# Three buffers instead of two for the attention inputs, with crossbar transfers issued one quad earlier

## The chip, the cores and the metric

The kernel runs on one core of a Trainium2 chip. The metric is the device time of one execution in microseconds (us); the time given for a kernel is the median of its runs.

## What is computed

The reference is a softcapped attention followed by a two-way maxout layer and an output projection. Cut to what matters:

```python
# q, k, v: (8 images, 12 heads, 448 rows, 64 columns), float32; cap = 30
scores = (q @ k^T) / sqrt(64)
scores = cap * tanh(scores / cap)
attn   = softmax(scores)
x      = attn @ v                      # as (3584, 768): images and rows by heads and columns
g      = maximum(x @ w1, x @ w2)       # w1, w2: (768, 1024)
out    = g @ w_out                     # (3584, 768), float32
```

## The kernel before

The 96 heads are taken as 48 pairs (index i), and two pairs make a quad (index t, 24 quads of four heads; pairs 2t and 2t+1). For each quad:

- **Loads.** The loads of k and q (steps `lk`, `lq`) go through GpSimd's queue (POOL in the profile), which turns float32 into bf16 on the way, into a constant tile `kqs[t % KB]`. v is loaded by `lv` into `vp[t % VB]` and, for the last 64 rows of a head, into `vl[t % VB]`.
- **Turning.** q and k have to stand with their 64 columns on the partitions. Pairs 0 to 9 (quads 0 to 4) are turned by TensorE (step `X`). From quad 5 on, the step `cr t` issues one transposing DMA through the crossbar from the queue of SyncE (SP), from `kqs[t % KB]` into the tile `qkT` of the quad, which comes from a pool of `QB` buffers.
- **Attention.** The scores are computed by `S i j` (three blocks of rows per pair) and `L t` (the rows that are left over); ScalarE (ACT) does tanh (`T`, `TL`) and exp (`E`, `EL`); VectorE (DVE) adds up the exponentials (`A`, `B`), and `Y` to `Y3` give the inverse sums. `VL t` and `V t` multiply by v, and `N t` normalizes into `xT`.
- **The layer.** maximum(h1, h2) is written as max(h1 - h2, 0) + h2, with w1 - w2 (`wd_sb`) and with w2 @ w_out (`wm_sb`) made once at the start. A group (`O` opens it, `M` steps it, `ev` evicts it) is one PSUM bank of output. `M x y n` steps two groups at a time: group x with the upper 64 rows of the contraction and group y with the lower 64, so that two matmuls of 64 rows each run side by side in the array. Between the two halves of a group stands a hand-over: a no-operation that waits for the last matmul of the first half and on which the first matmul of the second half waits. `Hs g` puts it on SP's queue, `H g` on DVE's. `st b t` issues the output stores, also on SP's queue.

The schedule is written out by hand: the string `ORDER` lists some 2,300 steps, and each engine takes its own instructions in just this order. Waits between engines come from the data: a load into a buffer waits for the last reader of what stood there, and a queue whose first instruction waits holds up all behind it. So a load for quad t waits, with two buffers, for the crossbar transfer of quad t-2 (`kqs`) or for the values of quad t-2 (`vp`, `vl`), and a transfer `cr t` waits for the loads of quad t and for the scores of quad t-2 (`qkT`).

In `ORDER`, `cr t` stands (from quad 6 on) beside the scores of pair 2t-2, one quad ahead of the quad that reads it. The loads of a quad stand ahead of its `cr`. The place that the change touches first, in the order before:

```python
M 19 17 1; M 19 18 1; T 15 0; N 6 0; M 19 18 2; lv 8 3; O 20 1; M 20 18 2; EL 7; Hs 19; ev 17; M 20 18 1; lk 20 0;
S 15 1; M 20 19 1; N 6 1; M 20 19 1; T 15 1; M 20 19 1; lk 20 1; O 21 2; M 21 19 3; Hs 20; M 21 20 1; lq 20 0;
```

Of the kernel before, what the change touches and what calls it, by code (L numbers as in the profile page):

```python
# [14 lines left out]
P 1 0 4; P 3 0 2; OP 2 0 3; P 2 0 7; P 1 0 1; P 2 0 1; P 1 0 1; P 3 0 2; P 1 0 2; PC 2 0; PC 1 0; E 1 2 3;
E 1 0 2; TL 1; T 2 0; EL 0; S 3 0; S 2 2; P 3 0 1; W 0 2; P 3 0 1; X 4 3; T 2 2; T 3 0; VL 0; Y 0 1; V 0 0 0 3;
V 0 1 0 3; S 3 1; lwo 1 0; lwo 1 1; lq 5 0; lk 5 0; lv 1 0; lv 1 1; lk 8 0; lq 8 0; lq 7 0; lw2 4; lv 6 2; lq 6 0;
lk 7 0; lk 6 0; lw2 5; lw1 2; lw1 4; lw1 0; lv 2 0; lv 2 1; WC 0; PC 3 0; XC 4; Y1 0; Y2 0; Y3 0; N 0 0; N 0 1;
E 2 0 3; T 3 1; EL 1; E 3 0 2; OP 0 0 1; P 0 0 2; OP 2 1 2; P 2 1 2; P 0 0 1; OP 1 1 3; P 1 1 2; P 0 0 1; P 1 1 2;
# [28 lines left out]
M 15 13 2; ev 12; M 15 13 1; lk 19 1; M 15 14 2; ev 13; M 15 14 1; T 14 0; O 16 1; M 16 14 1; lq 19 0; A 6 1 1;
M 16 14 1; st 0 1; M 16 14 1; Hs 15; T 14 1; cr 8; B 6 0; M 16 15 1; S 14 2; M 16 15 1; ev 14; M 16 15 1; T 14 2;
O 17 2; M 17 15 2; H 16; M 17 15 1; B 6 1; M 17 16 2; E 13 2 3; M 17 16 1; ev 15; O 18 3; M 18 16 1; L 7; VL 6;  # L50
A 6 1 2; st 0 2; TL 7; V 6 0 0 2; V 6 1 0 2; Y 6 0; E 14 0 3; V 6 0 2 3; V 6 1 2 3; Y1 6; S 15 0; M 18 16 1;
lv 8 0; M 18 16 1; Y2 6; M 18 17 1; Y3 6; M 18 17 1; lv 8 1; M 18 17 1; O 19 0; M 19 17 2; ev 16; Hs 18; lv 8 2;
M 19 17 1; M 19 18 1; T 15 0; N 6 0; M 19 18 2; lv 8 3; O 20 1; M 20 18 2; EL 7; Hs 19; ev 17; M 20 18 1; lk 20 0;
S 15 1; M 20 19 1; N 6 1; M 20 19 1; T 15 1; M 20 19 1; lk 20 1; O 21 2; M 21 19 3; Hs 20; M 21 20 1; lq 20 0;
ev 18; M 21 20 1; S 15 2; S 16 0; ev 19; M 21 20 1; T 15 2; O 22 3; M 22 20 1; lk 21 0; M 22 20 1; A 7 0 1; Hs 21;
# [723 lines left out]
```

## Time and profile before

| what | value |
|---|---|
| device time, median of 3 runs | 328.46 us (328.15 to 328.82) |
| span of the profiled execution, first to last instruction | 326.9 us |
| median less the span | 1.56 us |
| mean granted TensorE clock | 0.998 |
| busy: PE, ACT, DVE, POOL | 320.2, 281.1, 240.1, 162.2 us |
| crossbar transfers, time from issue to landing | 19, from 4.2 to 10.0 us, median 6.7 |

The profile comes from one execution, and its own device time is not among the three runs; its span is what stands for it, and the difference of 1.56 us to the median holds what lies around the span and whatever that execution did otherwise. PE is TensorE's matmuls and PEld its weight loads, which run beside matmuls. SPq and POOLq are the DMA queues of SP and POOL. In rows of the timeline and of the chain, the first number is the start in us from the span's start and the second is the length in us. The label `qkT<-kqs` marks a crossbar transfer, `kqs<-in_k_dram` and `kqs<-in_q_dram` the loads of k and q, `vp<-in_v_dram` and `vl<-in_v_dram` those of v. The row "DMA to landing" gives the time from the start of the issuing instruction to the last completion.

### The profile page before, as it was taken

To read this page: it belongs to the slowest core of one execution; us is meant where nothing else is said; L and a number is where in the kernel's file an instruction comes from. 1 tells how busy PE (TensorE), PEld (TensorE's weight loads), DVE (VectorE), ACT (ScalarE), POOL (GpSimd) and SP (SyncE) were. 2 spreads that over 40 slices of the span, in tenths; PEclk is the share of its full clock that TensorE was granted. 3 is DMA by queue.
4 is the path that set the end of the run, shared out by engine and by line. 5 is a ranking of instruction groups with operands and counts; after the bars stand their busy time and mean duration, and the time that the engine had idled before them with its cause. 6 is when DMAs were issued, how large, how long until landed. Compare 5 with 4: busy or idle time off the path is not lost.

```text
span 326.9 us, 9772 instructions
## 1 busy us (share of the span) xinstructions
PE 320.2 (98%) x4138; PEld 184.5 (56%) x4138; DVE 240.1 (73%) x422; ACT 281.1 (86%) x278; POOL 162.2 (50%) x237
## 2 busy tenths in 40 slices
PE   7999999999999999999999999999999999999994
PEld 3454545545656664565565565556466556557662
DVE  3346899987997778987897788968878779773201
ACT  5999999999999999999999999999999999921120
POOL 7357584568772772764774474478448311000000
PEclk9999999999999999999999999999999999999999
DMA  8999999899999999999999999999999963013033
GB/s 179 174 202 185 269 256 112 92 140 116 221 188 98 134 182 191 102 99 175 163 176 108 208 114 181 128 140 182 183 116 101 201 156 45 2 50 98 0 98 96
DMA packets 134508, 46.28 MB, mean 142 GB/s; under 512 B 112321, under 2 KB 129473, under 8 KB 134465
## 3 DMA queue, kind: packets, MB, share of 16 engines
q0 software_dynamic: 94592, 25.02, 78.3%
q1 hardware_dynamic: 39424, 19.99, 31.1%
q8 instruction: 32, 0.52, 0.6%
q10 hardware_dynamic: 448, 0.66, 0.5%
q14 instruction: 12, 0.09, 0.1%
HBM read 47.78 MB, written 11.01 MB: 180 GB/s over the span
## 4 chain that ended last, share of the span: by engine, by line
PE 93%; DMA 3%; POOL 1%; DVE 1%; issue 0%
PE mm L645 61%; PE s L514 9%; PE s L606 9%; PE mm L431 5%; DMA w2b<-in_moe_w_dram 3%; PE s L528 2%; PE s L600 2%; PE mm L573 2%; PE mm L640 1%; POOL kqs L321 1%; PE mm L458 1%; PE mm L566 1%; PE mm L416 0%; DVE xT L621 0%; POOL w2b L366 0%; DVE xT L618 0%
## 5 line engine op out<-in xcount | busy, mean ns | idle before, releaser
L519 ACT ACTIVATE e<-s 128x896 bf16<-128x896 f32 x144 | 125.5, 927 | 5.7 <-PE s L514 5.2
L536 ACT ACTIVATE e<-e 128x1792 bf16<-128x1792 bf16 (+2 forms) x72 | 122.7, 1709 | 0.0
L645 PE MATMUL mm<-wo_sb,gT 64*128 64x384 bf16 x864 | 115.2, 323 | 0.0
L645 PE MATMUL mm<-wm_sb,xT 64*128 64x384 bf16 x648 | 102.2, 323 | 0.0
L645 PE MATMUL mm<-xT,wd_sb 64*128 64x448 bf16 x768 | 97.5, 349 | 0.0
L328 POOL DMA_DIRECT2D kqs<-in_k_dram x76 | 54.7, 722 | 56.1 <-DMA qkT<-kqs 50.9
L645 PEld LDWEIGHTS <-gT 64*128 64x128 bf16 x864 | 58.6, 94 | 25.5 <-issue 1.1
L645 PEld LDWEIGHTS <-wd_sb 64*128 64x128 bf16 x768 | 48.8, 94 | 26.7 <-issue 2.1
L645 PEld LDWEIGHTS <-xT 64*128 64x128 bf16 x648 | 50.3, 94 | 18.5 <-issue 0.2
L514 PE MATMUL s<-qkT 64*128 64x448 bf16 x288 | 52.7, 352 | 0.2 <-DVE xT L618 0.2
L352 POOL DMA_DIRECT2D vp<-in_v_dram x48 | 30.5, 639 | 32.6 <-PE s L514 23.5
L666 DVE TENSOR_SCALAR gT<-mm 128x448 bf16<-128x448 f32 x64 | 38.9, 617 | 8.7 <-PE mm L645 7.6
L328 POOL DMA_DIRECT2D kqs<-in_q_dram x38 | 35.1, 924 | 5.7 <-issue 2.5
L606 PE MATMUL s<-e,vp 128*32 128x448 bf16 x576 | 36.1, 354 | 0.0
L548 DVE TENSOR_TENSOR esum<-e 128x896 bf16<-128x896 bf16 x42 | 25.9, 617 | 9.1 <-ACT e L536 9.1
L621 DVE TENSOR_TENSOR xT<-s,inv 64x448 bf16<-64x448 f32 x48 | 29.9, 622 | 1.7 <-PE s L606 0.8
L548 DVE TENSOR_TENSOR esum<-esum,e 128x896 bf16<-128x896 bf16 x42 | 26.2, 623 | 5.9 <-ACT e L536 4.8
L514 PEld LDWEIGHTS <-qkT 64*128 64x128 bf16 x288 | 18.5, 94 | 20.1 <-issue 12.0
L700 ACT COPY osb<-mm 128x384 f32<-128x384 f32 x10 | 4.8, 479 | 26.9 <-PE mm L645 26.7
L702 DVE COPY osb<-mm 128x384 f32<-128x384 f32 x44 | 23.3, 554 | 6.2 <-PE mm L645 5.7
L553 DVE TENSOR_TENSOR esum<-esum,el 64x896 bf16<-64x896 bf16 x42 | 26.0, 619 | 1.2
L578 DVE STREAM_TRANSPOSE st<-mm 128x448 f32<-128x448 f32 x24 | 15.6, 649 | 13.0 <-PE mm L573 11.3
(57 smaller groups left out, 269.7 us busy)
## 6 DMA issues: line engine op xcount, KB each, us to landing
out_dram<-osb SPq DMA_DIRECT2D x54, 192.0 KB, 4.5
vp<-in_v_dram POOLq DMA_DIRECT2D x38, 160.0 KB, 4.3
kqs<-in_q_dram POOLq DMA_DIRECT2D x46, 112.0 KB, 5.8
kqs<-in_k_dram POOLq DMA_DIRECT2D x76, 56.0 KB, 4.4
osb<-in_moe_w_dram POOLq DMA_DIRECT2D x4, 512.0 KB, 7.4
w2b<-in_moe_w_dram POOLq DMA_DIRECT2D x6, 256.0 KB, 7.1
wo_sb<-in_moe_w_out_dram POOLq DMA_DIRECT2D x4, 384.0 KB, 9.9
vp<-in_v_dram POOLq DMA_DIRECT2D x10, 128.0 KB, 7.7
```

What stands on the lines that cost most here:

```text
L328: nc.gpsimd.dma_start(out=to, in_=x)
L352: nc.gpsimd.dma_start(out=to, in_=x)
L514: scored[i, j] = nc.tensor.matmul(s[:, h, :S], k_of(t, o, h, j), q_of(t, o, h)).ins
L519: nc.scalar.activation(expo[i][:, 2 * j : 2 * j + 2, :], slots[i, j][:, :, :S], AF.Tanh, scale=scale / cap)
L536: nc.scalar.activation(e, e, AF.Exp, scale=float(cap))
L548: nc.vector.tensor_add(d, e[:, 0:2, :] if j == 1 else d, e[:, 2 * j : 2 * j + 2, :])
L553: nc.vector.tensor_add(d, d, left_e[t][r, :, :])
L606: nc.tensor.matmul(vals[t][place(m, u), u, :S], w[:, m, :], expo[2 * t + o][:, 2 * j + h, :], start=False, stop=(j == NJ - 1))
L621: nc.vector.tensor_mul(x[64 - r : 128 - r], vals[t][r : r + 64, u, :S], sums[t, 3][64 - r : 128 - r])
L645: ins = nc.tensor.matmul(self.ps, w[r], x[r], start=first, stop=self.at == [self.n, self.n]).ins
L666: nc.vector.tensor_relu(gT[b // 2][:, f, cs], ps)
L702: nc.vector.tensor_copy(o[:, hs], ps)
```

## The change

`KB`, `VB` and `QB` go from 2 to 3, so that `kqs`, `vp` and `vl`, and `qkT` have three buffers. All other steps keep their order; each `cr t` from quad 9 to quad 23 moves to the place at which `cr t-1` stood, and `cr 9` comes to a new place, between `Hs 19` and `ev 17`; the place of the former `cr 23` falls away. The condition in `transposes` is written in another way, with the same outcome at each of its calls. The lines of `ORDER` are wrapped anew, which is most of the diff; cut to its core:

```diff
@@ ORDER @@
 ...
-M 16 14 1; st 0 1; M 16 14 1; Hs 15; T 14 1; cr 8; B 6 0; M 16 15 1; S 14 2; M 16 15 1; ev 14; M 16 15 1; T 14 2;
+M 16 14 1; Hs 15; T 14 1; cr 8; B 6 0; M 16 15 1; S 14 2; M 16 15 1; ev 14; M 16 15 1; T 14 2; O 17 2;
 ...
+M 19 17 1; M 19 18 1; T 15 0; N 6 0; M 19 18 2; lv 8 3; O 20 1; M 20 18 2; EL 7; Hs 19; cr 9; ev 17; M 20 18 1;
 ...
-M 23 21 1; Hs 22; lq 21 0; M 23 21 1; M 23 22 2; ev 21; M 23 22 1; T 16 0; M 23 22 2; A 7 1 1; M 23 22 2; cr 9;
+M 23 22 2; cr 10; M 23 22 1; T 16 1; M 23 22 1; B 7 0; S 16 2; M 23 22 2; B 7 1; O 24 1; M 24 22 1; T 16 2;
 ...
-M 24 25 4; lq 23 0; M 24 25 3; T 18 0; O 27 0; M 27 25 1; A 8 1 1; M 27 25 1; cr 10; M 27 25 1; M 27 26 1; ev 24;
 ...
+lq 47 0; M 84 85 3; T 42 0; O 87 2; M 87 85 1; A 20 1 1; M 87 85 1; cr 23; M 87 85 1; M 87 86 1; ev 84;
 ...
-T 44 0; Hs 90; M 88 89 1; A 21 1 1; M 88 89 1; cr 23; M 88 89 2; B 21 0; M 88 89 1; T 44 1; M 88 89 1; S 44 2;
 ...
@@ the kernel @@
-    KB = 2
-    VB = 2
-    QB = 2
+    KB = 3
+    VB = 3
+    QB = 3
 ...
-        if c != 1:
+        if bank is not None:
             turned["qk", i] = mm_tile(bank).bitcast(bf16)
```

More of the change, by code (lines that the diff above doesn't have):

```diff
@@ L15 @@
[L15 to L19, printed above, removed]
@@ new lines @@
+W 3 2; W 2 1; T 1 0; T 1 2; lw2 1; lwo 0 0; lwo 0 1; lw2 0; lq 4 0; lk 4 0; lv 0 0; lv 0 1; XC 3; XC 2; WC 3;
+D 0 4; S 1 1; D 0 8; D 2 2; S 2 1; W 1 2; WC 2; WC 1; T 1 1; T 2 1; S 2 0; D 0 4; L 1; OP 3 0 0; P 3 0 2;
+OP 1 0 1; P 1 0 4; P 3 0 2; OP 2 0 3; P 2 0 7; P 1 0 1; P 2 0 1; P 1 0 1; P 3 0 2; P 1 0 2; PC 2 0; PC 1 0;
+E 1 2 3; E 1 0 2; TL 1; T 2 0; EL 0; S 3 0; S 2 2; P 3 0 1; W 0 2; P 3 0 1; X 4 3; T 2 2; T 3 0; VL 0; Y 0 1;
+V 0 0 0 3; V 0 1 0 3; S 3 1; lwo 1 0; lwo 1 1; lq 5 0; lk 5 0; lv 1 0; lv 1 1; lk 8 0; lq 8 0; lq 7 0; lw2 4;
@@ new lines @@
+lv 6 2; lq 6 0; lk 7 0; lk 6 0; lw2 5; lw1 2; lw1 4; lw1 0; lv 2 0; lv 2 1; WC 0; PC 3 0; XC 4; Y1 0; Y2 0;
+Y3 0; N 0 0; N 0 1; E 2 0 3; T 3 1; EL 1; E 3 0 2; OP 0 0 1; P 0 0 2; OP 2 1 2; P 2 1 2; P 0 0 1; OP 1 1 3;
+P 1 1 2; P 0 0 1; P 1 1 2; P 0 0 1; P 1 1 4; S 4 0; S 3 2; X 5 0; P 2 1 4; P 0 0 3; P 2 1 1; XC 5; PC 1 1;
+PC 0 0; T 3 2; T 4 0; E 3 2 3; OP 3 1 3; P 3 1 1; P 2 1 1; S 4 1; S 4 2; Y 1 1; T 4 1; T 4 2; L 2; P 3 1 4;
+VL 1; TL 2; V 1 1 0 3; V 1 0 0 3; S 5 0; X 6 0; E 4 0 3; T 5 0; EL 2; Y1 1; Y2 1; PC 2 1; Y3 1; N 1 1; N 1 0;
@@ new lines @@
+lk 10 0; lk 11 0; lk 11 1; lk 10 1; S 7 2; O 0 1; M 0 -1 2; S 7 1; M 0 -1 4; O 1 2; M 1 -1 1; T 7 2; T 7 1;
+Hs 0; M 1 -1 1; S 8 1; M 1 -1 1; M 1 0 3; S 8 0; X 9 3; OP 4 1 0; P 4 1 4; sub 1 0; sub 3 0; XC 9; T 8 1;
+E 7 0 2; T 8 0; E 7 2 3; P 4 1 4; L 4; O 2 3; M 2 0 3; S 8 2; M 2 1 3; A 3 1 1; B 3 1; PC 4 1; ev 0; B 3 0;
+Hs 2; TL 4; T 8 2; O 3 0; M 3 1 3; M 3 2 1; S 9 0; M 3 2 2; T 9 0; E 8 0 3; ev 1; A 3 1 2; sub 5 0; cr 5; Hs 3;
+O 4 1; M 4 2 1; VL 3; V 3 0 0 3; Y 3 2; V 3 1 0 3; M 4 2 2; S 9 1; M 4 3 3; lk 13 0; lk 13 1; lv 4 1; lv 4 0;
@@ new lines @@
+lv 5 3; lv 5 0; lq 13 0; lq 15 0; lq 12 0; lk 12 0; lk 15 1; Y1 3; Y2 3; Y3 3; ev 2; Hs 4; O 5 2; M 5 3 3;
+M 5 4 3; T 9 1; EL 4; ev 3; N 3 0; N 3 1; Hs 5; O 6 3; M 6 4 3; M 6 5 2; S 10 0; M 6 5 1; O 7 0; M 7 5 3; Hs 6;
+ev 4; A 4 0 1; ev 5; M 7 6 2; S 9 2; M 7 6 1; Hs 7; cr 6; E 9 0 2; T 10 0; T 9 2; O 8 1; M 8 6 3; S 10 2;
+M 8 7 3; S 10 1; O 9 2; M 9 7 1; T 10 2; T 10 1; E 9 2 3; M 9 7 2; VL 4; V 4 0 0 2; L 5; TL 5; A 4 1 1; H 8;
+A 4 0 2; B 4 1; ev 7; B 4 0; A 4 1 2; ev 6; M 9 8 3; V 4 1 0 3; Y 4 0; V 4 0 2 3; M 9 8 7; S 11 0; M 9 8 1;
@@ new lines @@
+O 10 3; M 10 8 3; E 10 0 3; T 11 0; EL 5; Hs 9; Hs 8 2; Y1 4; M 10 9 3; Y2 4; Y3 4; N 4 1; N 4 0; M 8 9 2;
+S 11 1; M 8 9 3; S 11 2; M 8 9 3; lv 5 2; lk 15 0; lk 14 0; lv 6 1; lk 14 1; lq 14 0; lv 5 1; lq 16 0; lv 6 3;
+lv 6 0; lk 16 1; lk 17 0; lk 16 0; T 11 1; T 11 2; E 11 0 2; O 11 0; M 11 9 3; S 12 0; M 11 10 6; S 12 1;
+M 11 10 1; ev 8; ev 9; A 5 0 1; A 5 0 2; lk 17 1; M 11 10 4; T 12 0; lq 17 0; O 12 1; M 12 10 1; A 5 1 1;
+M 12 10 1; Hs 11; cr 7; M 12 10 1; M 12 11 1; B 5 0; M 12 11 1; T 12 1; M 12 11 1; S 12 2; H 10 2; B 5 1;
@@ new lines @@
+M 25 24 1; N 7 1; M 25 24 2; lv 9 3; M 25 24 2; EL 8; M 25 24 1; S 17 1; lk 22 1; M 25 24 2; ev 22; M 25 24 1;
+T 17 1; S 17 2; lq 22 0; M 25 24 1; ev 23; M 25 24 1; O 26 3; M 26 24 1; T 17 2; M 26 24 1; A 8 0 1; Hs 25;
+S 18 0; M 26 24 1; lk 23 0; M 26 25 1; A 8 0 2; M 26 25 1; Hs 24 2; E 17 0 2; M 26 25 1; S 18 1; lk 23 1;
+M 24 25 1; Hs 26; M 24 25 4; lq 23 0; M 24 25 3; T 18 0; O 27 0; M 27 25 1; A 8 1 1; M 27 25 1; cr 11;
+M 27 25 1; M 27 26 1; ev 24; M 27 26 1; T 18 1; M 27 26 1; S 18 2; ev 25; M 27 26 2; T 18 2; M 27 26 1; B 8 0;
@@ new lines @@
+S 20 0; M 29 28 2; A 9 0 2; M 29 28 1; lk 25 0; E 19 0 2; O 30 3; M 30 28 1; S 20 1; M 30 28 1; Hs 29;
+M 30 28 1; lk 25 1; M 30 29 2; Hs 28 2; M 30 29 1; M 28 29 1; lq 25 0; M 28 29 1; T 20 0; Hs 30; M 28 29 1;
+A 9 1 1; M 28 29 1; cr 12; M 28 29 2; B 9 0; M 28 29 1; T 20 1; M 28 29 1; S 20 2; O 31 0; M 31 29 1; ev 28;
+M 31 29 1; T 20 2; M 31 29 1; B 9 1; M 31 30 3; st 1 5; E 19 2 3; ev 29; O 32 1; M 32 30 3; H 31; L 10; ev 30;
+VL 9; TL 10; V 9 0 0 2; A 9 1 2; V 9 1 0 2; E 20 0 3; M 32 31 1; Y 9 2; V 9 0 2 3; V 9 1 2 3; lk 26 0; Y1 9;
@@ new lines @@
+EL 11; lv 12 3; M 38 39 1; S 23 1; M 38 39 2; lk 28 1; A 11 0 1; M 38 39 1; T 23 1; S 23 2; M 38 39 2; A 11 0 2;
+lq 28 0; M 38 39 1; T 23 2; O 41 1; M 41 39 1; S 24 0; ev 38; M 41 39 2; M 41 40 1; lk 29 0; E 23 0 2;
+M 41 40 1; ev 39; S 24 1; M 41 40 2; lk 29 1; M 41 40 5; lq 29 0; M 41 40 1; T 24 0; M 41 40 1; A 11 1 1;
+O 42 2; M 42 40 1; cr 14; M 42 40 2; H 41; B 11 0; T 24 1; M 42 41 1; S 24 2; M 42 41 2; H 40 2; B 11 1;
+M 40 41 1; T 24 2; M 40 41 5; st 2 0; E 23 2 3; M 40 41 2; O 43 0; M 43 41 1; ev 40; L 12; VL 11; A 11 1 2;
@@ new lines @@
+TL 12; V 11 0 0 2; V 11 1 0 2; Y 11 3; E 24 0 3; V 11 0 2 3; V 11 1 2 3; Y1 11; S 25 0; lk 30 0; M 43 41 2;
+Y2 11; M 43 42 2; Y3 11; lv 13 0; M 43 42 4; N 11 0; lv 13 1; M 43 42 2; T 25 0; M 43 42 1; N 11 1; M 43 42 1;
+lv 13 2; M 43 42 1; O 44 3; M 44 42 2; EL 12; Hs 43; S 25 1; lv 13 3; M 44 42 1; M 44 43 1; ev 41; M 44 43 1;
+Hs 42 2; T 25 1; lk 30 1; S 25 2; M 44 43 1; A 12 0 1; M 42 43 2; Hs 44; lq 30 0; T 25 2; M 42 43 1; A 12 0 2;
+S 26 0; M 42 43 3; E 25 0 2; M 42 43 1; lk 31 0; S 26 1; M 42 43 1; O 45 1; M 45 43 2; ev 42; lk 31 1;
@@ new lines @@
+M 45 43 1; M 45 44 2; ev 43; M 45 44 1; T 26 0; lq 31 0; O 46 2; M 46 44 1; A 12 1 1; M 46 44 1; st 2 1;
+M 46 44 1; Hs 45; T 26 1; cr 15; B 12 0; M 46 45 1; S 26 2; M 46 45 1; ev 44; M 46 45 1; T 26 2; O 47 0;
+M 47 45 2; H 46; M 47 45 1; B 12 1; M 47 46 2; E 25 2 3; M 47 46 1; ev 45; O 48 3; M 48 46 1; L 13; VL 12;
+A 12 1 2; st 2 2; TL 13; V 12 0 0 2; V 12 1 0 2; Y 12 1; E 26 0 3; V 12 0 2 3; V 12 1 2 3; Y1 12; S 27 0;
+M 48 46 1; lv 14 0; M 48 46 1; Y2 12; M 48 47 1; Y3 12; M 48 47 1; lv 14 1; M 48 47 1; O 49 1; M 49 47 2; ev 46;
@@ L166 @@
[L166 removed]
+M 52 50 1; lk 33 0; M 52 50 1; A 13 0 1; Hs 51; M 52 50 1; M 52 51 1; E 27 0 2; M 52 51 1; lk 33 1; ev 50;
+S 28 1; M 52 51 1; O 53 1; M 53 51 1; A 13 0 2; M 53 51 1; Hs 52; lq 33 0; M 53 51 1; M 53 52 2; ev 51;
+M 53 52 1; T 28 0; M 53 52 2; A 13 1 1; M 53 52 2; cr 16; M 53 52 1; T 28 1; M 53 52 1; B 13 0; S 28 2;
+M 53 52 2; B 13 1; O 54 2; M 54 52 1; T 28 2; M 54 52 2; H 53; M 54 53 1; H 52 2; E 27 2 3; M 54 53 2;
@@ new lines @@
+M 52 53 1; L 14; VL 13; A 13 1 2; TL 14; V 13 0 0 2; V 13 1 0 2; Y 13 0; E 28 0 3; V 13 0 2 3; lk 34 0;
+V 13 1 2 3; Y1 13; S 29 0; M 52 53 1; lv 15 0; M 52 53 1; Y2 13; M 52 53 2; Y3 13; M 52 53 1; lv 15 1;
+M 52 53 2; O 55 0; M 55 53 1; N 13 0; M 55 53 1; lv 15 2; M 55 53 1; T 29 0; M 55 54 1; N 13 1; M 55 54 2;
+lv 15 3; M 55 54 2; EL 14; M 55 54 1; S 29 1; lk 34 1; M 55 54 2; ev 52; M 55 54 1; T 29 1; S 29 2; lq 34 0;
+M 55 54 1; ev 53; M 55 54 1; O 56 3; M 56 54 1; T 29 2; M 56 54 1; A 14 0 1; Hs 55; S 30 0; M 56 54 1; lk 35 0;
@@ new lines @@
+M 56 55 1; A 14 0 2; M 56 55 1; Hs 54 2; E 29 0 2; M 56 55 1; S 30 1; lk 35 1; M 54 55 1; Hs 56; M 54 55 4;
+lq 35 0; M 54 55 3; T 30 0; O 57 1; M 57 55 1; A 14 1 1; M 57 55 1; cr 17; M 57 55 1; M 57 56 1; ev 54;
+M 57 56 1; T 30 1; M 57 56 1; S 30 2; ev 55; M 57 56 2; T 30 2; M 57 56 1; B 14 0; M 57 56 4; B 14 1; st 3 3;
+E 29 2 3; M 57 56 1; O 58 2; M 58 56 2; L 15; VL 14; A 14 1 2; TL 15; V 14 0 0 2; V 14 1 0 2; Y 14 0; E 30 0 3;
+V 14 0 2 3; V 14 1 2 3; Y1 14; lk 36 0; st 3 4; S 31 0; M 58 56 1; M 58 57 1; Y2 14; M 58 57 1; Hs 56 2;
@@ new lines @@
+cr 18; M 58 59 2; B 15 0; M 58 59 1; T 32 1; M 58 59 1; S 32 2; O 61 1; M 61 59 1; ev 58; M 61 59 1; T 32 2;
+M 61 59 1; B 15 1; M 61 60 3; st 3 5; E 31 2 3; ev 59; O 62 2; M 62 60 3; H 61; L 16; ev 60; VL 15; TL 16;
+V 15 0 0 2; A 15 1 2; V 15 1 0 2; E 32 0 3; M 62 61 1; Y 15 0; V 15 0 2 3; V 15 1 2 3; lk 38 0; Y1 15; S 33 0;
+M 62 61 2; Y2 15; lv 17 0; O 63 3; M 63 61 1; st 3 6; Y3 15; M 63 61 2; Hs 62; lv 17 1; M 63 62 1; T 33 0;
+N 15 0; M 63 62 2; lv 17 2; O 64 0; M 64 62 1; ev 61; M 64 62 1; Hs 63; EL 16; M 64 62 1; S 33 1; lv 17 3;
@@ new lines @@
+M 71 70 1; ev 69; S 36 1; M 71 70 2; lk 41 1; M 71 70 5; lq 41 0; M 71 70 1; T 36 0; M 71 70 1; A 17 1 1;
+O 72 0; M 72 70 1; cr 20; M 72 70 2; H 71; B 17 0; T 36 1; M 72 71 1; S 36 2; M 72 71 2; H 70 2; B 17 1;
+M 70 71 1; T 36 2; M 70 71 5; st 4 0; E 35 2 3; M 70 71 2; O 73 1; M 73 71 1; ev 70; L 18; VL 17; A 17 1 2;
+TL 18; V 17 0 0 2; V 17 1 0 2; Y 17 3; E 36 0 3; V 17 0 2 3; V 17 1 2 3; Y1 17; S 37 0; lk 42 0; M 73 71 2;
+Y2 17; M 73 72 2; Y3 17; lv 19 0; M 73 72 4; N 17 0; lv 19 1; M 73 72 2; T 37 0; M 73 72 1; N 17 1; M 73 72 1;
@@ new lines @@
+lv 19 2; M 73 72 1; O 74 3; M 74 72 2; EL 18; Hs 73; S 37 1; lv 19 3; M 74 72 1; M 74 73 1; ev 71; M 74 73 1;
+Hs 72 2; T 37 1; lk 42 1; S 37 2; M 74 73 1; A 18 0 1; M 72 73 2; Hs 74; lq 42 0; T 37 2; M 72 73 1; A 18 0 2;
+S 38 0; M 72 73 3; E 37 0 2; M 72 73 1; lk 43 0; S 38 1; M 72 73 1; O 75 2; M 75 73 2; ev 72; lk 43 1;
+M 75 73 1; M 75 74 2; ev 73; M 75 74 1; T 38 0; lq 43 0; O 76 0; M 76 74 1; A 18 1 1; M 76 74 1; st 4 1;
+M 76 74 1; Hs 75; T 38 1; cr 21; B 18 0; M 76 75 1; S 38 2; M 76 75 1; ev 74; M 76 75 1; T 38 2; O 77 1;
@@ new lines @@
+Hs 80; M 81 79 1; M 81 80 1; lq 44 0; ev 78; M 81 80 1; S 39 2; S 40 0; ev 79; M 81 80 1; T 39 2; O 82 3;
+M 82 80 1; lk 45 0; M 82 80 1; A 19 0 1; Hs 81; M 82 80 1; M 82 81 1; E 39 0 2; M 82 81 1; lk 45 1; ev 80;
+S 40 1; M 82 81 1; O 83 2; M 83 81 1; A 19 0 2; M 83 81 1; Hs 82; lq 45 0; M 83 81 1; M 83 82 2; ev 81;
+M 83 82 1; T 40 0; M 83 82 2; A 19 1 1; M 83 82 2; cr 22; M 83 82 1; T 40 1; M 83 82 1; B 19 0; S 40 2;
+M 83 82 2; B 19 1; O 84 0; M 84 82 1; T 40 2; M 84 82 2; H 83; M 84 83 1; H 82 2; E 39 2 3; M 84 83 2;
@@ new lines @@
+M 82 83 1; L 20; VL 19; A 19 1 2; TL 20; V 19 0 0 2; V 19 1 0 2; Y 19 1; E 40 0 3; V 19 0 2 3; lk 46 0;
+V 19 1 2 3; Y1 19; S 41 0; M 82 83 1; lv 21 0; M 82 83 1; Y2 19; M 82 83 2; Y3 19; M 82 83 1; lv 21 1;
+M 82 83 2; O 85 1; M 85 83 1; N 19 0; M 85 83 1; lv 21 2; M 85 83 1; T 41 0; M 85 84 1; N 19 1; M 85 84 2;
+lv 21 3; M 85 84 2; EL 20; M 85 84 1; S 41 1; lk 46 1; M 85 84 2; ev 82; M 85 84 1; T 41 1; S 41 2; lq 46 0;
+M 85 84 1; ev 83; M 85 84 1; O 86 3; M 86 84 1; T 41 2; M 86 84 1; A 20 0 1; Hs 85; S 42 0; M 86 84 1; lk 47 0;
@@ L202 @@
+ev 118; M 119 119 12; ev 119; st 7 6;
 """
```

271 lines of the change are left out of this document (95 added, 176 removed).

## Prediction

> **What bounds the kernel now.** I read the profile's page first, then the waits, then the chain in order of time.
>
> ```profile
> PE 320.2 (98%) x4138; PEld 184.5 (56%) x4138; DVE 240.1 (73%) x422; ACT 281.1 (86%) x278; POOL 162.2 (50%) x237
> PE   7999999999999999999999999999999999999994
> PE 93%; DMA 3%; POOL 1%; DVE 1%; issue 0%
> PE mm L471 <- DVE warm L734: 1.8, 1, 1.8
> PE mm L416 <- DMA w2b<-in_moe_w_dram: 0.5, 1, 0.5
> PE s L514 <- DVE xT L618: 0.2, 1, 0.2
> POOL kqs L328 <- DMA qkT<-kqs: 52.5, 14, 6.3
> POOL vp L352 <- PE s L514: 23.5, 6, 9.5
> 102.25 0.87 PE s L606 x16
> 172.58 0.87 PE s L606 x16
> 242.91 0.87 PE s L606 x16
> ```
>
> TensorE is busy for 320.2 of 326.9 us, and of the 6.7 us left the waits explain 2.5 (1.8 + 0.5 + 0.2). None of the three is for a crossbar transfer, for loaded q, k or v, or for SP. The three rows of the chain are the values step at the same point of three rounds of six quads: the distance is 70.33 us both times, 11.72 us a quad. A wait for a DMA, whose landing times vary, would make rounds differ. The long waits, 52.5 and 23.5 us, are POOL's, for buffers that the change doubles up on. They are real and they go; but nobody on the chain waits for POOL. So the change takes away waits that cost nothing, and what it can do to the time has to come from what its earlier transfers and its moved SP instructions run into.
>
> **Part 1: loads start earlier.** The first time that the third buffer matters is here, in POOL's timeline:
>
> ```profile
> 52.61 0.62 POOL L352 DMA_DIRECT2D vl<-in_v_dram  x1 [0.46 <-DMA kqs<-in_k_dram]
> 58.51 0.62 POOL L352 DMA_DIRECT2D vp<-in_v_dram  x1 [5.29 <-PE s L606]
> 59.13 0.96 POOL L328 DMA_DIRECT2D kqs<-in_q_dram  x1
> 62.37 1.84 POOL L328 DMA_DIRECT2D kqs<-in_q_dram  x2 [2.29 <-issue]
> 54.00:56.00 2.00, 2.00 (x24) 1.09 (x22) 1.94 (x5) 2.00 (x4) 0.00 (x0) 1.00 0.23 20
> ```
>
> The load of v for quad 5 waits until 58.51 for the values of quad 3, which read `vp[1]`. With three buffers it goes into `vp[2]`, free since quad 2, so POOL goes on at 53.23 (52.61 + 0.62). The loads behind it (q and k of quads 6 and 7) find their buffers free as well, so that nine of them, at 0.62 to 0.96 us each, fill the stretch from 53.2 to about 60. The last row is a window (its last two columns are DMA share and GB/s): before, the DMA engines were nearly idle there, at 0.23 and 20 GB/s.
>
> Into just this gap falls the first crossbar transfer, `cr 5`, which stays where it is:
>
> ```profile
> 55.25 1.58 SPq L475 DMA_TRANSPOSE qkT<-kqs  x1
> DMA to landing us min/median/max: 5.3/5.3/5.3
> 61.16 0.10 PEld L514 LDWEIGHTS <-qkT 64*128 64x128 bf16 x2
> 98.26 1.30 SPq L475 DMA_TRANSPOSE qkT<-kqs  x1
> DMA to landing us min/median/max: 6.2/6.2/6.2
> 168.54 1.48 SPq L475 DMA_TRANSPOSE qkT<-kqs  x1
> DMA to landing us min/median/max: 6.7/6.7/6.7
> 67.85 1.86 SPq L475 DMA_TRANSPOSE qkT<-kqs  x1
> DMA to landing us min/median/max: 5.0/5.0/5.0
> 75.82 2.20 SPq L475 DMA_TRANSPOSE qkT<-kqs  x1
> DMA to landing us min/median/max: 7.8/7.8/7.8
> 262.60 1.48 SPq L475 DMA_TRANSPOSE qkT<-kqs  x1
> DMA to landing us min/median/max: 4.2/4.2/4.2
> DMA to landing us min/median/max: 4.2/6.7/10.0
> ```
>
> Each row of an issue has its landing below it; the last line is for all 19. `cr 5` is issued at 55.25 and lands at 60.55; its first reader, the weight load of `S 10 0`, comes at 61.16. The slack is 0.61 us, so any landing time over 5.9 us stops TensorE. With loads in flight and no stores behind them, transfers took 6.2 and 6.7 us (98.26 and 168.54) and 5.0 (67.85); 7.8 with some stores (75.82); the one without any loads took 4.2. I take 6.5, between the two nearest rows: 55.25 + 6.5 = 61.75, a stop of 0.6 us. Below, at 5.0, it is nothing; above, at 7.8, it is 1.9, and at the 10.0 of the worst transfer 4.1. It can't fall below nothing, since TensorE does not wait there now. TensorE has no idle time later in which to win it back, so it goes to the end in full.
>
> The Trainium skill (DMA: Bandwidth & Descriptors, section "Queues, rings and completion order") says that each DMA engine goes in turn through the queue rows that have work, one packet from each. This speaks against the change: a crossbar transfer whose row was alone would get half the turns. By it, what the 4.2 us of the lone transfer hold beyond its 1.48 us of issuing would double: 1.48 + 2 x 2.72 = 6.9 us, an estimate; the stop would be 1.0 us and the sum 0.4 us higher. The trace goes part of the way: 6.2 and 6.7 us with loads, against 4.2 without.
>
> For the later quads the third buffer only moves work that has a cover. POOL is busy for half of the span (50% on the page) and gains a quad's lead. The scores of quad 9 start so late after its transfer:
>
> ```profile
> 107.94 0.35 PE L514 MATMUL s<-qkT 64*128 64x448 bf16 x1
> 73.04 0.11 PEld L514 LDWEIGHTS <-qkT 64*128 64x128 bf16 x2
> ```
>
> `cr 9` lands at 98.26 + 6.2 = 104.5 and is read at 107.9. A quad earlier makes 3.5 us of slack into some 15: worth nothing, as nobody waits. `cr 6` (67.85 + 5.0 = 72.85, read at 73.04) has only 0.19 us of slack; after the change its loads, held up before behind the wait at 58.51, come some 5 us sooner, and it gets several us. That is worth nothing in this execution; what it is worth in others is a rival below.
>
> **Part 2: the transfers move on SP's queue.** From `cr 10` on, each transfer takes the exact place of its predecessor, with the same wait for scores (quad t-3 in place of t-2, one place earlier), and with the loads a quad ahead. What is behind it on SP is what was behind the former one. I count this at nothing; the cover is that the loads have landed (third rival). One place is new: `cr 9` behind `Hs 19`. Behind it on SP stands `Hs 20`, the hand-over for which the first matmul of group 20's second half waits.
>
> ```profile
> L654 SPq EVENT_SEMAPHORE  x1: 17/17/17, 93.9 to 93.9; - x1
> L654 SPq EVENT_SEMAPHORE  x1: 17/17/17, 95.3 to 95.3; - x1
> 95.44 0.10 PEld L645 LDWEIGHTS <-wd_sb 64*128 64x128 bf16 x2
> L654 SPq EVENT_SEMAPHORE  x1: 17/17/17, 54.9 to 54.9; - x1
> 88.21 0.91 POOL L328 DMA_DIRECT2D kqs<-in_q_dram  x1 [0.25 <-issue]
> L475 SPq DMA_TRANSPOSE qkT<-kqs x19: 1296/1655/2655, 55.3 to 262.6; - x19
> ```
>
> `Hs 19` runs at 93.9 and `Hs 20` at 95.3; the weight load that needs the latter comes at 95.44. A transfer starts about 0.3 us behind the hand-over ahead of it (54.9 and 55.25 for `cr 5`, where several semaphores are read in between), so `cr 9` starts at 94.2. It holds SP for 1.30 to 2.66 us, at the median 1.66. So SP is free at 95.86, and `Hs 20` reaches TensorE at about 95.9 in place of 95.3: a stop of 0.5 us. The ends are 0.1 us (1.30) and 1.5 us (2.66). Its loads are no question: the last of them was issued at 88.21 before, and comes earlier with the lead of part 1; and its buffer of `qkT` was last read by quad 6.
>
> **Part 3: the rest.** The new condition in `transposes` gives the same calls. The number of matmuls, activations, loads and bytes is the same. SP's place for the last transfer falls away behind the last quads, where SP has nothing due. All of this is nothing.
>
> **The sum.** In the profiled execution 0.6 + 0.5 = 1.1 us: a span of 328.0 in place of 326.9. The median of the runs lies 1.56 us above the span; with the same distance it goes from 328.46 to 329.6 us, 0.3% slower. About 0.2% (0.66 us, also the spread of the three runs before) is what a measurement of this kernel can tell from no change.
>
> **The rivals.**
>
> *Covered (no change).* If `cr 5` lands within 5.9 us, as the 5.0 of the transfer at 67.85 did with loads around it, and `cr 9` holds SP near its shortest 1.30 us, the sum is 0.1 to 0.6 us, and the time 328.5 to 329.0. For it: both margins are missed by little in the middle case. Against it: both have to go well together.
>
> *A stop that the profiled execution did not have (faster).* `cr 6` made its reader by 0.19 us with the second shortest landing I quote, 5.0. If in the timed runs it usually takes the median 6.7, `S 12 0` stops for 67.85 + 6.7 - 73.04 = 1.5 us in them, and this is part of the 1.56 us above the span. After the change `cr 6` no longer waits for late loads, and the stop is gone. With parts 1 and 2 at their small ends (0 and 0.1 to 0.5) the time is 327.1 to 327.5. It decides where the landing of `cr 6` passes 5.2 us. For it: the slack of 0.19 is hardly luck-proof. Against it: the three runs lie within 0.67 us. The Trainium skill (Trainium Kernel Development and Optimization, section "Performance Expectations") warns that a busy matmul row is a bad measure, as matmuls are pipelined; by it short waits could hide in the 98%. The equal rounds of 70.33 us speak against any but in the first third.
>
> *SP waits for loads (much slower).* If POOL does not get its lead by `cr 10`, that transfer waits at SP at 98.26 for the last load of quad 10, which before was issued only then:
>
> ```profile
> 98.21 0.91 POOL L328 DMA_DIRECT2D kqs<-in_q_dram  x1
> kqs<-in_q_dram POOLq DMA_DIRECT2D x46, 112.0 KB, 5.8
> ```
>
> It would block SP for 5.8 us, and hand-overs and stores behind it stop TensorE for some 2 to 5 us, each quad again until POOL has caught up: 332 us or more. Against it: its buffer is free when `cr 7` has landed, at 83.6 (75.82 + 7.8) at the latest, and six loads of q and k and four of v need about 7 us of POOL, so that it is landed by 97.
>
> **How the numbers follow.** The forecast (a stop of 0.66 to 3 us) has 0.52, the third rival 0.05, the covered case 0.28, the faster one 0.15. Slower is 0.52 + 0.05 = 0.57. The predicted time is that of the likeliest case, 329.6. The range starts at 327.6, in the faster case, and ends at 331.6, which is 3.1 us more than before: most of the bounds 1.9 + 1.5 together. About 0.1 is left out on each side.
>
> **What would show it right or wrong.** Right: POOL's load of v for quad 5 starts at 53.2 and not at 58.5; the landing of `cr 5` is over 5.9 us, and the waits list TensorE's scores waiting for a crossbar transfer, once, for about 0.6 us; one hand-over (`Hs 20`) comes right behind a transfer on SP near 95.9; from there on all rounds are still 70.33 us; POOL no longer waits for `qkT<-kqs`. Wrong: `cr 5` within 5.9 us (part 1), SP done with `cr 9` by 95.4 (part 2), rounds shorter than 70.33 us (then the steady state had hidden waits after all), or SP waiting for loads at a transfer.

## The result and the profile after

The changed kernel takes 332.36 us (median of 4 runs, 330.65 to 332.54) and the kernel before, in runs on the same chip, 328.55 us: a ratio of 1.0105, with a 95% interval of 1.0081 to 1.0129. So it is about 1% slower; the medians differ by 3.8 us. The forecast was 329.6 us in a range up to 331.6: the direction is right, the size is not. A run that is more than 1.5% above the fastest of its kernel is left out of the ratios (one run each of extra, held and before_vb3 below).

The page of the profiled execution (332.25 us, span 330.5 us): busy times and the chain by engine. All line numbers of the changed kernel lie four above those of before: L518 is the scores, L479 the crossbar transfer, L356 the load of v.

```profile
PE 320.2 (97%) x4136; PEld 184.2 (56%) x4138; DVE 240.3 (73%) x422; ACT 281.2 (85%) x278; POOL 161.6 (49%) x237
...
PE 87%; DMA 9%; POOL 1%; DVE 1%; issue 0%
```

The waits of the same execution (us in all, times, longest):

```profile
PEld L518 <- DMA qkT<-kqs: 3.5, 2, 3.0
PE s L518 <- DMA qkT<-kqs: 2.5, 1, 2.5
PE mm L435 <- DMA wo_sb<-in_moe_w_out_dram: 1.4, 1, 1.4
POOL vp L356 <- PE s L518: 67.7, 15, 9.0
POOL kqs L332 <- DMA qkT<-kqs: 7.3, 2, 6.7
```

TensorE does the same work, 320.2 us, in a span that is 3.6 us longer. DMA had 3% of the chain and has 9%, and there is a new wait: the scores for a crossbar transfer. The matmuls of the scores lose 2.5 us in one stop. POOL's waits did what the change says: those for `qkT<-kqs` shrink from 52.5 to 7.3 us, while those for `vp` grow from 23.5 to 67.7, since POOL, a quad further ahead, now stops there. On the chain POOL has 1%, before and after.

Where on the way the time goes is found by taking each matmul's start in the one trace from its start in the other. The changed kernel is 0.72 us late from 16.8 us on, 3.38 from the first scores of quad 5 (`S 10 0`), 3.56 from those of quad 6 (`S 12 0`), and 3.56 to the end. The first step is the wait for `wo_sb` above; it is chance and does not come from the third buffers, for at 22 us, behind the same place, kernels with three buffers below are 0.38 (nomove), 0.37 (held) and 0.79 us (early6) early. The 2.66 us at `S 10 0` are the bulk of the cost; `S 12 0` adds 0.3 (the matmuls win back 0.1 in between). POOL's timeline after:

```profile
53.32 0.64 POOL L356 DMA_DIRECT2D vp<-in_v_dram  x1
53.93 0.96 POOL L332 DMA_DIRECT2D kqs<-in_q_dram  x1
55.11 1.84 POOL L332 DMA_DIRECT2D kqs<-in_q_dram  x2 [0.22 <-PE s L518]
56.95 1.40 POOL L332 DMA_DIRECT2D kqs<-in_k_dram  x2
58.34 0.62 POOL L356 DMA_DIRECT2D vl<-in_v_dram  x1
58.96 1.46 POOL L332 DMA_DIRECT2D kqs<-in_k_dram  x2
```

The issue of `cr 5` and its landing:

```profile
L479 SPq DMA_TRANSPOSE qkT<-kqs x1: 1965/1965/1965, 55.9 to 55.9; - x1
DMA to landing us min/median/max: 8.7/8.7/8.7
```

The timeline of the weight load that reads it, and one window (busy us of PE, PEld, DVE, ACT and POOL, then granted clock, DMA share and GB/s):

```profile
64.73 0.10 PEld L518 LDWEIGHTS <-qkT 64*128 64x128 bf16 x2 [2.97 <-DMA qkT<-kqs]
```

```profile
62.00:64.00 2.00, 0.20 (x4) 0.00 (x0) 1.96 (x4) 1.08 (x1) 0.72 (x1) 1.00 1.93 151
```

The loads come one behind the other from 53.3 us on, where before POOL stood still until 58.5. `cr 5` is under way beside them and takes 8.7 us in place of 5.3. TensorE is busy for 0.20 us of the two from 62 to 64.

How many packets of POOL's queue (q0; packets, then MB) the DMA engines moved between issue and landing of `cr 5`, before and after (DMA views of 55.25 to 60.55 and of 55.94 to 64.64):

```profile
q0 software_dynamic: 40, 0.03, 7.3%
```

```profile
q0 software_dynamic: 4049, 0.58, 102.2%
```

### The profile page after: what moved, and what is told of

It is laid out like the page before. It is cut to its first block, busy times and chain, and to the rows that moved or that the text cites. A ratio compares the mean times of both kernels' runs of the same rounds, so it can differ in the third digit from the quotient of the medians.

```text
span 330.5 us, 9759 instructions
## 1 busy us (share of the span) xinstructions
PE 320.2 (97%) x4136; PEld 184.2 (56%) x4138; DVE 240.3 (73%) x422; ACT 281.2 (85%) x278; POOL 161.6 (49%) x237
## 4 chain that ended last, share of the span: by engine, by line
PE 87%; DMA 9%; POOL 1%; DVE 1%; issue 0%
PE mm L649 57%; PE s L518 9%; PE s L610 8%; DMA qkT<-kqs 6%; PE mm L435 5%; DMA wo_sb<-in_moe_w_out_dram 3%; PE s L532 2%; PE s L604 1%; PE mm L644 1%; PE mm L577 1%; POOL kqs L325 1%; PE mm L462 1%; PE mm L570 1%; POOL w2b L370 0%; DVE xT L625 0%; PE mm L420 0%
## 5 line engine op out<-in xcount | busy, mean ns | idle before, releaser
L356 POOL DMA_DIRECT2D vp<-in_v_dram x48 | 30.4, 637 | 73.1 <-PE s L518 67.7
L518 PE MATMUL s<-qkT 64*128 64x448 bf16 x288 | 52.8, 353 | 2.8 <-DMA qkT<-kqs 2.5
L518 PEld LDWEIGHTS <-qkT 64*128 64x128 bf16 x288 | 18.5, 94 | 23.4 <-issue 12.0
```

The source lines that it names most:

```text
L356: nc.gpsimd.dma_start(out=to, in_=x)
L518: scored[i, j] = nc.tensor.matmul(s[:, h, :S], k_of(t, o, h, j), q_of(t, o, h)).ins
```

## The experiments

The theory: the third buffers take away POOL's waits, and these waits had kept loads off `cr 5`; the loss is that transfer, slowed by the loads beside it. Rivals: the moved transfers cost (on SP's queue, or by waiting there for loads), or the third buffers cost in some other way.

**nomove**: three buffers, transfers at their old places (`cr 9` behind `M 23 22 2`, and so on).

```diff
-M 20 18 2; EL 7; Hs 19; cr 9; ev 17;
+M 20 18 2; EL 7; Hs 19; ev 17;
...
-M 23 22 2; cr 10; M 23 22 1;
+M 23 22 2; cr 9; M 23 22 1;
```

> The changed kernel's three buffers of everything, with the transfers left at their old places. Theory A: as slow as the changed kernel, 331.5 to 332.5 us, with the first transfer landing in about 8 to 9 us and the scores of pair 10 waiting some 2.5 us for it. Rival B: 328.4 to 329.3 us.

Measured: 332.69 us (331.91 to 333.0), ratio 1.0127 (1.0110 to 1.0143). The same transfer with the same landing, and the wait for it:

```profile
L475 SPq DMA_TRANSPOSE qkT<-kqs x1: 2328/2328/2328, 54.9 to 54.9; - x1
DMA to landing us min/median/max: 8.7/8.7/8.7
PEld L514 <- DMA qkT<-kqs: 3.0, 1, 3.0
```

The windows around that stop (busy us of PE, PEld, DVE, ACT and POOL, then granted clock, DMA share and GB/s):

```profile
60.35:63.76 3.41, 0.89 (x12) 0.29 (x8) 2.88 (x5) 1.67 (x2) 1.55 (x2) 1.00 1.84 162
63.76:67.17 3.41, 3.41 (x20) 1.41 (x20) 1.16 (x2) 1.26 (x2) 3.02 (x5) 0.50 1.80 163
```

The moved transfers are not the cost: without them the kernel is as slow. And something more shows: behind the stop, which ends at 63.7, the granted clock is 0.50 for 3.4 us, and the matmuls fall back by another 1.6 us (from 2.31 late at `S 10 0` to 3.88).

**moveonly**: transfers moved, `KB` and `VB` back to 2 (`QB` stays 3). **vb2**: the changed kernel with `VB = 2` alone.

```diff
-    KB = 3        # moveonly only
+    KB = 2
-    VB = 3        # moveonly and vb2
+    VB = 2
```

> The kernel before with the transfers at their new places and three buffers of the turned tiles, but two of loaded k and q and of v. Theory A alone: the first two transfers land as before, nothing is lost before 90 us. The third rival of the prediction then adds what it costs when a transfer finds its loads not landed: the transfer of quad 10 waits on SP from about 98 to 104 us, and hand-overs behind it stop TensorE for 1 to 5 us, perhaps in each later quad: 330 to 340 us. If that rival is wrong, 328.4 to 329 us. Rival B: about 332 us, with the cost at quad 9 and 10 and none before.

> The changed kernel with v back at two buffers (VB = 2), k, q and turned tiles at three, transfers at their new places. Theory A (loads that no longer wait for the values of quad 3 run into the first two crossbar transfers, and TensorE waits for them): POOL stops again until about 58.5 us for the load of v of quad 5, the first transfer lands in 5 to 6 us, the second in 5 to 7, the scores wait for neither, and the time is 328.4 to 329.3 us. Rival B (the moved transfers cost it, by holding SP or by meeting loads later on): still 331.5 to 332.5 us, with two or more us lost after 90 us. Rival C (the start itself got slower by 0.7 us with the third buffer): 0.7 us is lost before 20 us here too, 329.2 to 330 us.

Measured: moveonly 341.71 us, ratio 1.039 (1.0357 to 1.0424); vb2 341.10 us, 1.038 (1.0341 to 1.0419). SP's and TensorE's waits in moveonly, and then in vb2:

```profile
SPq L479 <- DMA kqs<-in_k_dram: 31.9, 12, 6.5
SPq L479 <- DMA kqs<-in_q_dram: 28.1, 17, 5.7
...
PE mm L649 <- SPq L658: 9.4, 6, 2.6
```

```profile
SPq L479 <- DMA kqs<-in_k_dram: 31.1, 12, 6.9
SPq L479 <- DMA kqs<-in_q_dram: 26.2, 16, 5.3
...
PEld L649 <- SPq L658: 11.4, 6, 3.3
```

In both `cr 5` has its gap again (landings of 5.3 and 4.9 us, no stop at `S 10 0`). But the transfers now come to SP ahead of their loads, SP stands for 57 to 60 us in all, and behind it wait the hand-overs, and TensorE for them, from 95.6 us on. In moveonly these waits make 9.4 of the 14.1 us by which the span is longer, and with two of the stops the granted clock falls to 0.50 for 3.41 us each (from 119.87 and from 270.05), which makes some 3.3 us more, an estimate. So the move is not safe without the third buffer of v: with it missing, POOL stops at `vp` and the loads of q and k behind it are late. Whether the move also needs the third buffer of k and q was not tried: no run has the move with `KB = 2` and `VB = 3`. The expectation for vb2 (328.4 to 329.3) had only half of this: the early stop goes, but I had not seen that v's buffers carry the lead of q and k, which stand in the same queue. moveonly came out 1.7 us above its expected 330 to 340.

**before_vb3** and **kb3**: the kernel before with one number changed, `VB = 3` in the one and `KB = 3` in the other.

> The kernel before with three buffers of v alone (KB = 2, QB = 2). Theory A: POOL goes on at 53.2 us with the load of v of quad 5 and one load of q, then stops for the buffer of k and q that the first transfer reads; so only two loads meet the first transfer, it lands in 5.5 to 7 us, and TensorE waits 0 to 1 us: 328.4 to 329.8 us. Rival B: as before, 328.3 to 328.8 us. Rival C (third buffer of v slows the start): 0.7 us lost before 20 us, 329.2 us or more.

> The kernel before with three buffers of loaded k and q alone (VB = 2, QB = 2, transfers at their old places). POOL still stops until 58.5 us for the values of quad 3, so the first transfer lands in 5 to 6 us and nobody waits for it. Theory A: then the loads of quads 6 and 7 run without a stop, meet the second transfer (issued at about 67 us), it lands in 7.5 to 10 us in place of 5.0, and the scores of pair 12 wait 1 to 3.5 us for it: 329.5 to 332.5 us. Rival (only v's third buffer costs): 328.3 to 328.9 us.

Measured: kb3 328.59 us, ratio 1.0005 (0.9996 to 1.0014): nothing. before_vb3 332.93 us (the runs in the ratio: 329.26 to 332.99), ratio 1.0101 (1.0042 to 1.0159), with three stops in place of one:

```profile
PEld L514 <- DMA qkT<-kqs: 5.7, 3, 2.3
```

Both missed their expectations, kb3 below and before_vb3 above. kb3 shows why: a load of v that waits for `vp` keeps q and k off, as before (`cr 5` lands after 4.9 us, `cr 6` after 4.2). In before_vb3 it is the other wait, for `kqs`, that keeps `cr 5` free (5.4 us). Only in the kernels with both gone does `cr 5` meet the loads. What stops before_vb3 is `cr 6` (7.5 us in place of 5.0) and, later, `cr 14` (9.9) and `cr 20` (10.8). This reads like chance of landings with little slack behind them, as the spread of its runs does, but one trace can't show it; why just these took so long is open.

**extra** and **extra2**: the kernel before with seven loads more (three of q, four of k) into a spare tile, before the load that waits for the values of quad 3. This adds the loads and changes no buffer. In extra the rows of the spare tile were contiguous, in extra2 scattered like those of `kqs`.

```diff
-lk 13 1; lv 4 1; lv 4 0; lv 5 3; lv 5 0; lq 13 0;
+lk 13 1; lv 4 1; lv 4 0; lv 5 3; dx 0; dx 1; dx 2; dx 3; dx 4; dx 5; dx 6; lv 5 0; lq 13 0;
```

> The kernel before (two buffers, transfers at their old places) with seven added loads of q and k into a spare tile that nobody reads, between the loads of v for quad 5, so that POOL is busy from 53.2 to about 59 us as it is in the changed kernel. Theory A (loads in flight slow the first transfer): it lands in 8 to 9 us in place of 5.3, the scores of pair 10 wait 2 to 3 us for it, and the time is 330.5 to 333 us. Rival (it comes with three buffers as such, their addresses or waits, and not with loads in flight): landing 5 to 6 us, 328.3 to 329 us.

> The kernel before, two buffers and old places, with seven loads added (three of q, four of k, in the same shape and with the same scattered rows as the loads of q and k) between the last two loads of v for quad 5, into spare tiles that nobody reads. They run while cr 5 is on its way. If it is loads in flight that slow a transposing transfer (theory), cr 5 lands after 7.5 to 9 us in place of 5.3, S 10 0 stops for 1.5 to 3 us, perhaps with 1.6 us of slow clock behind it: 330 to 333.5 us. If the third buffers cost by themselves (rival), nothing changes: 328.3 to 329.0.

Measured: extra 328.80 us, ratio 1.0008 (0.9999 to 1.0017), a miss that decides nothing: in few long rows the loads made only 486 packets of POOL's queue between issue and landing of `cr 5`, which landed after 5.3 us. extra2 329.76 us (329.32 to 332.36), ratio 1.0049 (1.0027 to 1.0071). Its `cr 5`, then POOL's queue from issue to landing, then the waits:

```profile
L487 SPq DMA_TRANSPOSE qkT<-kqs x1: 2547/2547/2547, 54.9 to 54.9; - x1
DMA to landing us min/median/max: 7.6/7.6/7.6
```

```profile
q0 software_dynamic: 3664, 0.46, 104.4%
```

```profile
PEld L526 <- DMA qkT<-kqs: 2.1, 2, 1.8
PE s L526 <- DMA qkT<-kqs: 1.4, 1, 1.4
```

With two buffers and every transfer at its old place, loads in flight alone slow `cr 5` from 5.3 to 7.6 us and stop the scores for 1.4 us. About 1 of the 2.3 us lies in the issuing instruction itself (2.55 us in place of 1.58; it is 1.97 in the changed kernel and 2.33 in nomove). It is the same loss, if smaller than the 8.7 us and 2.5 us of the changed kernel; the median is just below what was expected, 330.

**held** and **held_nomove**: the other way about, three buffers but the loads held back by hand. A no-operation on POOL waits for the values of quad 3 ahead of most loads (`gv 3`), and a second until `cr 6` has landed (`gc 6`). held is the changed kernel, held_nomove has the transfers at their old places.

```diff
-lk 13 0; lk 13 1; lv 4 1; lv 4 0; lv 5 3; lv 5 0; lq 13 0; lq 15 0; lq 12 0; lk 12 0; lk 15 1;
+lk 13 0; lk 13 1; lv 4 1; lv 4 0; lv 5 3; gv 3; lq 13 0; lq 12 0; lk 12 0; lv 5 0; lq 15 0; lk 15 1;
...
-lv 5 2; lk 15 0; lk 14 0; lv 6 1; lk 14 1; lq 14 0;
+lv 5 2; lk 15 0; lk 14 0; gc 6; lv 6 1; lk 14 1; lq 14 0;
```

> The changed kernel (three buffers, moved transfers) with two holds on POOL: after the loads for quad 4 it waits for the values of quad 3 (as with two buffers of v), then loads q and k of quad 6 first; and ahead of the last loads for quad 7 it waits until the second transfer has landed. Theory A: the first two transfers land in 5 to 6.5 us, no score waits for them, POOL gets its lead later on, and the moved transfers cost at most 0.2 us: 328.2 to 329.2 us, no different from the kernel before by more than 0.2%. Rival B (something else in the changed kernel costs 3 us): 331 us or more. If the two-buffer kernel has stops in its timed runs that its profile lacks (a rival of the prediction), 327.0 to 327.8 us.

> Three buffers, transfers at their old places, and POOL held twice: until the values of quad 3 before most of the loads of quads 5 to 7, and until cr 6 has landed before the loads of v for quad 6. Theory: the whole cost of the three buffers is that loads run beside cr 5 and cr 6; with both holds, neither stops TensorE, and as the transfers are at their old places they have no lead to lose: 328.2 to 329.0 us, no wait of the scores for a transfer, none of SP for loads. Rival (something else in the three buffers costs too): 331 or more.

Measured: held 332.04 us, ratio 1.0095 (1.0080 to 1.0111); held_nomove 331.25 us (329.98 to 332.39), ratio 1.0081 (1.0058 to 1.0104). Both miss. `cr 5` is free in both (5.0 and 5.1 us), and `S 10 0` and `S 12 0` do not stop. But the second hold makes the loads of quad 7 late, and in held those of later quads too. The waits of held, and those of held_nomove:

```profile
SPq L483 <- DMA kqs<-in_k_dram: 6.0, 3, 2.8
SPq L483 <- DMA kqs<-in_q_dram: 4.9, 5, 2.4
...
PE mm L657 <- SPq L666: 2.2, 2, 1.1
PEld L526 <- DMA qkT<-kqs: 0.9, 1, 0.9
```

```profile
SPq L479 <- DMA kqs<-in_q_dram: 3.3, 2, 2.9
PEld L522 <- DMA qkT<-kqs: 1.2, 1, 1.2
PE s L614 <- DMA vp<-in_v_dram: 1.0, 1, 1.0
```

In held the moved transfers come to SP ahead of their loads, and two hand-overs behind them stop TensorE for 2.2 us, at 97.7 and 119.3: the cost of moveonly on a small scale. In both `cr 7` waits for its loads, lands late and stops `S 14 0`, and in held_nomove a load of v stops the values of quad 5. By themselves these two left the rival open, that three buffers cost in some other way too.

**early6**: the changed kernel with one hold only, and with the loads of quad 6 ahead of it, so that the lead stays.

```diff
-lk 13 0; lk 13 1; lv 4 1; lv 4 0; lv 5 3; lv 5 0; lq 13 0; lq 15 0; lq 12 0; lk 12 0; lk 15 1;
+lk 13 0; lk 13 1; lq 13 0; lq 12 0; lk 12 0; gv 3; lv 4 1; lv 4 0; lv 5 3; lv 5 0; lq 15 0; lk 15 1;
```

> The changed kernel with moved transfers and one hold: the loads of q and k for quad 6 are issued at once, and POOL then waits for the values of quad 3 before the loads of v for quads 4 and 5 and all behind. There is no second hold, so that the lead for cr 9 and later stays. Theory: cr 5 lands within 5.9 us and S 10 0 does not stop; cr 6, ready at its place, still shares with loads and S 12 0 stops for 0 to 1 us; nothing later: 328.2 to 329.5 us. Rival (the moved transfers cost something by themselves, or the lead is lost again): 331 or more.

Measured: 328.71 us (327.95 to 329.69, 12 runs) beside 328.54 us before (20 runs), ratio 1.0006 (0.9995 to 1.0017). POOL's timeline, then `cr 5` and `cr 6` with their landings, then the chain:

```profile
51.67 0.73 POOL L332 DMA_DIRECT2D kqs<-in_k_dram  x1 [0.60 <-issue]
58.00 1.26 POOL L356 DMA_DIRECT2D vp<-in_v_dram  x2 [5.60 <-PE mm L657]
```

```profile
L483 SPq DMA_TRANSPOSE qkT<-kqs x1: 1584/1584/1584, 54.5 to 54.5; - x1
DMA to landing us min/median/max: 4.9/4.9/4.9
L483 SPq DMA_TRANSPOSE qkT<-kqs x1: 1730/1730/1730, 62.7 to 62.7; - x1
DMA to landing us min/median/max: 5.6/5.6/5.6
```

```profile
PE 97%; DMA 1%; DVE 1%; issue 0%
```

All three third buffers, all moved transfers, and no cost: the scores wait for no transfer any more. So the loss of the changed kernel comes from the loads issued between 53 and 60 us, and what else the change may cost lies within the interval, which ends at 0.2%. It also gains nothing, though SP never waits for loads of q and k in it.

## Why the prediction was right in its mechanism and wrong in its size

**What bounds the kernel** held: early6 keeps one hold of POOL but has most of the freed waits (5.0 us for `qkT<-kqs` in place of 52.5) without the collision, and is as fast as before. POOL's waits for buffers were worth nothing to the chain.

**Part 1** named the right place and the right mechanism: POOL's load of v for quad 5 starts at 53.32 (53.2 was predicted), `cr 5` is slowed and `S 10 0` stops once. The step that failed is the size of its one term, the landing of `cr 5`. I took a landing of 6.5 us from two rows of the steady state (6.2 and 6.7) and got a stop of 0.6 us; the landing was 8.7, here and in nomove, and the stop 2.66 us. That lies above the 1.9 us that I had put into the range, and inside the 4.1 us that the worst transfer of before (10.0) gave and that I left out. Part of the error is in the choice of rows: I took over what other transfers need with loads, where `cr 5` needs 5.3 us already with next to none and the last transfer 4.2. The 2.0 to 2.5 us by which 6.2 and 6.7 lie above 4.2 make 7.3 to 7.8 on top of its own 5.3, a stop of 1.4 to 1.9 us, an estimate; what made up the last us is open. The estimate by turns of the Trainium skill (DMA: Bandwidth & Descriptors, section "Queues, rings and completion order"), 6.9 us, was too small for the same reason: worked out from `cr 5`'s own row, 1.58 us of issuing and 3.72 behind it, it is 1.58 + 2 x 3.72 = 9.0 us, an estimate, and the 8.7 measured lie below it. The number of load packets beside the transfer does not settle the size either. POOL's queue from issue to landing of the transfer of before that took 6.7 us (168.54 to 175.24):

```profile
q0 software_dynamic: 3566, 0.45, 112.2%
```

That is 532 packets for each us, more than the 465 of the 8.7 us after (4,049 in all). That loads slow it is shown; why by 1.4 us in one case and by 3.4 in another is not.

`cr 6` was to get several us of slack and did not. Its loads are early, but its place on SP is behind `Hs 7`, at 62.7 (early6), and after the stop at 66.9. There it met the loads too, landed after 9.8 us and stopped `S 12 0` for 0.3 us:

```profile
L479 SPq DMA_TRANSPOSE qkT<-kqs x1: 2597/2597/2597, 66.9 to 66.9; - x1
DMA to landing us min/median/max: 9.8/9.8/9.8
```

I had looked at the loads that it waited for and not at the next thing that it waits for.

**Part 2** priced `cr 9` at 0.5 us, with 0.1 at the short end; it cost nothing that shows in the lateness of the matmuls. The transfer held SP for 1.30 us from 97.79 on, and the hand-over behind it ran at 99.1. That is no luck: in all twelve traces `cr 9` holds SP for 1.29 to 1.37 us, and the row at 98.26 (1.30) that I quoted is `cr 9` itself, where I took the median of all 19. From `cr 10` on, and in **part 3**, nothing was predicted and nothing came. The chain's values step after, at the points that were quoted for before:

```profile
105.82 0.87 PE s L610 x16
176.15 0.87 PE s L610 x16
246.48 0.87 PE s L610 x16
```

The rounds are 70.33 us both times, as before: all of the loss comes in the first third.

**The sum** was 1.1 us of span. It came out at 3.6: 2.66 for `cr 5`, 0.3 for `cr 6`, less the 0.1 won back between them, nothing for `cr 9`, and 0.7 of chance at 16.8 us. What the sum had no term for is the clock behind a stop. It stayed at 1.00 in this execution; in nomove it cost 1.6 us more. Of the three timed runs of the changed kernel beside the profiled one, two have a mean granted clock of 0.993 and 0.995 (332.54 and 332.46 us) and one of 1.000 (330.65 us); 3.4 us at half of the clock would lower the mean of 330 us by 0.005, so the slow clock is likely part of the two, though no trace of them shows it. The lower end of the range, 327.6, was put "in the faster case", but lies above that case's own 327.1 to 327.5; nothing came of it.

**The rivals.** The covered case (landing within 5.9 us) did not come; early6 is what it would have been. The faster one, that `cr 6` stops unseen in the timed runs before, falls: early6 is rid of any such stop and no faster. The third, SP waiting for loads, did not come with this change, as the lead is there by `cr 9`; moveonly and vb2 show that it costs 12 to 13 us where the lead is missing, far above the least that I named for it (332 us).

## What to carry to other kernels

A wait that costs the chain nothing may still be a schedule: before it is taken away, ask what the freed queue will start, and what transfer with little slack is under way at that moment. Price such a transfer with loads beside it from its own landing without them, and by the upper part of the landings, not by two rows near their median, when its slack is 0.6 us and the landings reach 10. And when a deeper buffer only brings forward what nobody waits for, it can be paired with a hold that keeps the old gap (early6), but then it has nothing to give either.

## What was not expected of the hardware

- A stop of 2.5 us can cost more than itself. In nomove the scores waited for 2.52 us, and the granted clock was then 0.50 from 63.76 to 67.17 us: 1.6 us more. In the changed kernel they waited for 2.53 us and the clock stayed at 1.00. What differs is where the stop lies. In each of the twelve traces all changes of the clock lie whole multiples of 3.413 us apart. Such a stretch of nomove holds its whole stop and leaves TensorE 0.89 us of work (row above). In the changed kernel, counted back from its next change of clock at 329.96 us, a boundary at 63.72 cuts the stop in two:

```profile
60.31:63.72 3.41, 1.89 (x20) 0.77 (x16) 3.35 (x6) 2.77 (x3) 1.46 (x3) 1.00 1.52 143
63.72:67.13 3.41, 2.40 (x27) 1.46 (x29) 1.78 (x4) 1.58 (x2) 2.57 (x4) 1.00 1.96 153
```

In moveonly and vb2 the clock is halved twice each, behind stretches with 0.66 to 1.32 us of work; from 10 us on, no trace shows it halved behind one with 1.8 or more. The Trainium skill (TensorE: Matmul & The Clock Gate, section "What's actually happening") has a free-running window of some 3.4 us, and half the clock after an idle one; the length and the free running agree with these rows, but here the window need not be idle throughout.
- The same transposing transfer of one quad landed after 3.4 to 10.8 us in these traces. With fewer than 60 load packets beside it, it took 3.4 (several of moveonly and vb2) to 5.3 us (`cr 5` of before); among the longest, the number of load packets in flight does not order them.
